# Writing and reading the two halves of one PSUM bank together: a Strassen-type channel layer in four turns instead of five

## The chip, the cores and the metric

The kernel runs on one core of a Trainium2 chip, with five engines that run side by side and meet at semaphores: TensorE (PE in the profile, with its weight loads listed apart as PEld), VectorE (DVE), ScalarE (ACT), GpSimd (POOL) and SyncE (SP), which issues the DMAs. The metric is the device time of one execution in microseconds; less is better.

## The reference

Three layers follow each other, all in fp32: a windowed attention, a gated channel mix, and a block that mixes along the sequence and then along the channels. The change touches only the last of them.

```python
def _moe2_ref(x, U, V, w_ch1, w_ch2) -> np.ndarray:
    xt = x.transpose(0, 2, 1)
    h = xt @ U @ V
    u = x + h.transpose(0, 2, 1)
    ch = np.maximum(u @ w_ch1, 0.0) @ w_ch2
    return (u + ch).astype(np.float32)
```

Here `x` is 4 x 576 x 512, `w_ch1` is 512 x 2048 and `w_ch2` is 2048 x 512. The "first channel layer" is `u @ w_ch1` with its relu, the "second" is the product with `w_ch2`.

## The kernel before

**Products.** Each fp32 product is made of three matmuls in a faster format: an operand is split into a high part (a copy that ACT rounds) and a low part (the rest, a subtraction on DVE or POOL), and high x high, low x high and high x low are added up in PSUM. The helper `part_split` does a split: `part_hi` on ACT, `part_lo` on the engine that it is given.

**Groups and pairs.** The 2304 tokens are cut into one group of 256 (g = 0) and four groups of 512 (g = 1 to 4), the 2048 hidden channels into eight blocks j of 256. The work runs over pairs (g, j), 40 in all, in the order of `VISITS`: four blocks of each group, then all eight of group 4, then the other four blocks of groups 3, 2, 1 and 0. For the 32 pairs with g of 1 or more a pair is a 2 x 2 block product, done by Winograd's form of Strassen's method with seven products of quarter size instead of eight. `ch1(g, j)` makes the first layer of a pair, `ch2(g, j, ...)` the second, one pair later. The eight pairs of group 0 (`ch1_first`) have two products for each layer.

**The first layer of a pair.** Its seven products of six matmuls (128 x 128 by 128 x 256) all go through one PSUM bank of 512 columns, half 0 or half 1 (`at_`). Products are accumulated on top of what the halves hold, and between them DVE or ACT read the partial sums. Before the change each read takes one half (256 columns): `taken` copies product 2 to p2 on ACT; `relu_sum` (line 1264) and `less` (line 1269) on DVE make h11, p5, u2, t3 and h22; the last read is h21 on ACT (line 1292). Then follow sums and splits that make the operands of the second layer.

**The second layer of a pair.** Seven products, each added into its own bank (`ACC`, seven banks), so that of PSUM's eight banks one is left to the first layer. A product is one operation of six matmuls, three for each half m.

**The operands of a group.** Before a visit `x_steps` makes seven operands of the group: three plain blocks (`x_plain`) and the sums T1, T2, T4 and T3 (`x_sum`, `more`), each with a split whose low part runs on POOL (`X_ENG`).

**The order of the work.** All operations are put into a list with the keys that they read and write, and a planner in the kernel (`plan`) simulates them with estimated durations, tries 84 orders and takes the best. An operation of PE is a whole product; the planner puts one where its keys are free. Before the change the keys of the two halves are apart, `(acc, 0)` and `(acc, 1)`. The framework below sets the semaphores by itself, from the tiles that each instruction touches, in the order that the planner wrote.

Of the kernel before, what the change touches and what calls it, by code (L numbers as in the profile page):

```python
# [15 lines left out]
ALU = mybir.AluOpType  # L16
# [3 lines left out]
P = 128  # L20
# [52 lines left out]
LATER = {(0, 0): ((2, 1), (2, 2), (3, 2)), (4, 2): ((4, 1), (4, 2)), (4, 3): ((5, 1), (5, 2)), (4, 4): ((6, 1), (6, 2)), (4, 5): ((7, 1), (7, 2))}  # L73
VISITS = tuple((g, 0, 4) for g in range(4)) + ((4, 0, 8),) + tuple((g, 4, 8) for g in (3, 2, 1, 0))
PRESUM = 6
W_ENG, X_ENG, H_ENG = (("DVE",) * 4, ("DVE",) * 4), "POOL", "DVE"
W_TAG = ("rt k2", "pt pt", "w32 w32")
FLT_MAX = 3.4028235e38
# [23 lines left out]
def tile_attention_mix_channel(  # L102
# [431 lines left out]
    def part_split(eng, x, hi, lo):  # L534
        part_hi(x, hi)
        part_lo(eng, x, hi, lo)
# [86 lines left out]
    def weight(j, layer, name):  # L623

        n, c = (AT1 if layer == 1 else AT2)[name]
        p = wparts[j]
        return cut(p[n, "h"], c, c + Q), cut(p[n, "l"], c, c + Q)
# [526 lines left out]
    def x_plain(g, name, k, t):  # L1154
        x_slot(g, name)
        part_split(X_ENG, ublocks[g, k, t], *operands[g, name])
# [3 lines left out]
    def x_sum(g, name, a, b):  # L1160
        x_slot(g, name)
        t = tt[g, name] = loose("y", 2, "tt")
        part_sum(t, a, b, ALU.subtract)
        part_split(X_ENG, t, *operands[g, name])

    def x_steps(g):

        def ub(k, t):
            return ublocks[g, k, t]

        def more(name, of, last):
            x_slot(g, name)
            t = tt[g, name] = tt[g, last]
            part_sum(t, of, t, ALU.subtract)
            part_split(X_ENG, t, *operands[g, name])

        if g == 0:
            return [
                lambda: (load_block(0, 0, 0), load_block(0, 1, 0)),
                lambda: x_plain(0, "1", 0, 0),  # L1180
                lambda: x_plain(0, "2", 1, 0),
                lambda: x_sum(0, "d", ub(1, 0), ub(0, 0)),
            ]
        return [
            lambda: [load_block(g, k, t) for t, k in ((0, 1), (0, 0), (1, 0), (1, 1))],
            lambda: x_plain(g, "21", 1, 0),
            lambda: x_sum(g, "T1", ub(0, 1), ub(0, 0)),
            lambda: x_plain(g, "11", 0, 0),
            lambda: more("T2", ub(1, 1), "T1"),
            lambda: x_plain(g, "22", 1, 1),  # L1190
            lambda: more("T4", ub(1, 0), "T2"),
            lambda: x_sum(g, "T3", ub(1, 1), ub(0, 1)),
        ]
# [5 lines left out]
    def ch1_bank(g, j):  # L1199
        return fixed_bank("M", 3 if g or j % 2 == 0 else 2)  # L1200

    def ch1_product(g, j, acc, at_, trips, start, keys):

        wx = [(weight(j, 1, w), operands[g, x]) for w, x in trips]

        def run():
            a = acc()[:, at_ * Q : (at_ + 1) * Q]
            n = 0
            for (wh, wl), (xh, xl) in wx:
                for i in range(2):  # L1210
                    ci, wi = (i * Q, (i + 1) * Q), (i * P, (i + 1) * P)
                    n += 1
                    last = n == 2 * len(wx)
                    nc.tensor.matmul(a, lhsT=wh(*wi), rhs=xh(*ci), start=start and n == 1, stop=False, skip_group_check=True)  # L1214
                    nc.tensor.matmul(a, lhsT=wl(*wi), rhs=xh(*ci), start=False, stop=False, skip_group_check=True)  # L1215
                    nc.tensor.matmul(a, lhsT=wh(*wi), rhs=xl(*ci), start=False, stop=last, skip_group_check=True)  # L1216

        r = [k for (wh, wl), (xh, xl) in wx for y in (wh, wl, xh, xl) for k in y.keys()]
        pe(6 * len(wx) * MMQ, run, r + keys[0], [(acc, at_)] + keys[1], "f32r")

    H_LOW = {"a": 0, "b": 2, "t": 4, "c": 5}
    H_HIGH = (
# [8 lines left out]
    def ch1_first(j):  # L1231

        acc = ch1_bank(0, j)
        ch1_product(0, j, acc, 0, (("11", "1"), ("12", "2")), True, ([], [(acc,)]))
        ch1_product(0, j, acc, 1, (("S1", "1"), ("22", "d")), True, ([], [(acc,)]))
        x = {k: part(*v) for k, v in H_FIRST[j % 2].items()}
        pair, t = loose("pr", 2, "hp"), loose("pr", 1, "ht")
        act(2 * Q, lambda: nc.scalar.activation(pair.words(), acc(), AF.Relu), [(acc,), (acc, 0), (acc, 1)], pair.keys(), psum=True)
        part_sum(t, cut(pair, Q, 2 * Q), cut(pair, 0, Q), ALU.subtract)
        part_split(H_ENG, pair, x["ph"], x["pl"])  # L1240
        part_split(H_ENG, t, x["th"], x["tl"])
        return {
            "1": (cut(x["ph"], 0, Q), cut(x["pl"], 0, Q)), "2": (cut(x["ph"], Q, 2 * Q), cut(x["pl"], Q, 2 * Q)), "d": (x["th"], x["tl"])}

    def ch1(g, j):
        if g == 0:
            return ch1_first(j)
        acc = ch1_bank(g, j)
        fresh = (acc, "start")
        hi = {k: part(*v) for k, v in H_HIGH[j % 2].items()}  # L1250
        lo = {k: part("x", j % 2, H_LOW[k], hi[k].n // Q) for k in hi}
        a, b, c, p25 = loose("pr", 2, "ha"), loose("pr", 2, "hb"), loose("sig", 4, "hc"), loose("m", 2, "p25")
        h11, t1, h22, t3 = cut(a, 0, Q), cut(a, Q, 2 * Q), cut(b, 0, Q), cut(b, Q, 2 * Q)
        t2, h21, t4, u2 = (cut(c, i * Q, (i + 1) * Q) for i in range(4))
        p2, p5 = cut(p25, 0, Q), cut(p25, Q, 2 * Q)

        def product(n, at_, start):
            ch1_product(g, j, acc, at_, (USES[n],), start, ([], [fresh, (acc, 0)]) if start else ([fresh], []))

        def taken(to, at_):  # L1260
            copy(Q, lambda: to.words(), lambda: acc()[:, at_ * Q : (at_ + 1) * Q], [(acc, at_)], to.keys(), psum=True)

        def relu_sum(to, at_, more):
            dve(Q, lambda: nc.vector._custom_dve(  # L1264
                TENSOR_ADD_SAT, out=to.words(), in0=acc()[:, at_ * Q : (at_ + 1) * Q], in1=more.words(), s0=FLT_MAX, s1=0.0),
                [(acc, at_)] + more.keys(), to.keys(), two=True, psum=True)

        def less(to, at_, b):
            dve(Q, lambda: nc.vector.tensor_tensor(  # L1269
                out=to.words(), in0=acc()[:, at_ * Q : (at_ + 1) * Q], in1=b.words(), op=ALU.subtract),  # L1270
                [(acc, at_)] + b.keys(), to.keys(), two=True, psum=True)

        product(2, 1, True)
        taken(p2, 1)
        product(1, 0, False)
        relu_sum(h11, 0, p2)
        product(5, 1, False)
        less(p5, 1, p2)
        product(6, 0, False)
        less(u2, 0, p2)  # L1280
        product(3, 1, False)
        relu_sum(t3, 1, u2)
        product(7, 0, False)
        part_sum(t1, t3, h11, ALU.subtract)
        relu_sum(h22, 0, p5)
        product(4, 0, False)
        part_split(H_ENG, a, hi["a"], lo["a"])
        part_sum(t3, h22, t3, ALU.subtract)
        part_sum(t2, h22, t1, ALU.subtract)
        part_split(H_ENG, b, hi["b"], lo["b"])  # L1290
        part_split(H_ENG, t2, hi["t"], lo["t"])
        act(Q, lambda: nc.scalar.activation(h21.words(), acc()[:, :Q], AF.Relu), [(acc, 0)], h21.keys(), psum=True)
        part_sum(t4, h21, t2, ALU.subtract)
        part_split(H_ENG, cut(c, Q, 3 * Q), hi["c"], lo["c"])
        at_ = {"11": ("a", 0), "T1": ("a", 1), "22": ("b", 0), "T3": ("b", 1), "T2": ("t", 0), "21": ("c", 0), "T4": ("c", 1)}
        return {n: tuple(cut(z[k], i * Q, (i + 1) * Q) for z in (hi, lo)) for n, (k, i) in at_.items()}
# [4 lines left out]
    def ch2_product(j, acc, trips, hid, first, last):  # L1301
        wx = [(weight(j, 2, w), hid[x]) for w, x in trips]

        def run():
            for m in range(2):
                a = acc()[:, m * Q : (m + 1) * Q]
                wi = (m * P, (m + 1) * P)
                for i, ((wh, wl), (xh, xl)) in enumerate(wx):
                    start, stop = first and m == 0 and i == 0, last and i == len(wx) - 1
                    nc.tensor.matmul(a, lhsT=wh(*wi), rhs=xh(), start=start, stop=False, skip_group_check=True)  # L1310
                    nc.tensor.matmul(a, lhsT=wl(*wi), rhs=xh(), start=False, stop=False, skip_group_check=True)  # L1311
                    nc.tensor.matmul(a, lhsT=wh(*wi), rhs=xl(), start=False, stop=stop, skip_group_check=True)  # L1312

        r = [k for (wh, wl), (xh, xl) in wx for y in (wh, wl, xh, xl) for k in y.keys()]
        pe(6 * len(wx) * MMQ, run, r, [(acc,)], "f32r")

    def ch2(g, j, hid, first, last, h):
        if g == 0:
# [315 lines left out]
```

## Time and profile before

| | us |
|---|---|
| median of three runs (787.13 to 788.87) | 788.27 |
| the profiled execution, its own time | 785.79 |
| its span in the profile | 783.9 |

The span is what the profile covers, from the first instruction to the last; 1.9 us of the execution lie around it. Matmuls are pipelined, so the profile's busy time of PE counts overlaps, and the distance from one matmul's start to the next says more. The first products of the channel layers start at 343.9 us of the span; from about 400 us on nothing else runs on PE but the two channel layers.

### The profile page before, as it was taken

How to read it: one execution, taken by the hardware profiler on the slowest of the kernel's cores; microseconds unless marked ns; L12 is line 12 of the kernel's file. 1: busy time of each engine (PE TensorE's matmuls, PEld its weight loads, DVE VectorE, ACT ScalarE, POOL GpSimd, SP SyncE). 2: the span in 40 equal slices, each digit the busy share in tenths (PEclk: the TensorE clock that was granted, in tenths of full speed). 3: DMA queues.
4: the chain of work that ended last, by engine and by line, in shares of the span. 5: the costliest groups of instructions: out<-in, count | busy, mean ns of one | idle time of the engine just before them, and what ended most of it. 6: DMA issues, size and time to landing. Idle time of an engine off the chain costs nothing.

```text
span 783.9 us, 19194 instructions
## 1 busy us (share of the span) xinstructions
PE 739.7 (94%) x7498; PEld 697.4 (89%) x7498; DVE 590.5 (75%) x1502; ACT 402.0 (51%) x1017; POOL 202.3 (26%) x219
## 2 busy tenths in 40 slices
PE   8999999999989999988989889999999999989998
PEld 6778999999989999977879879888888899889997
DVE  5879988877676547899866888768887778676853
ACT  6888977676857454745424323244554333243321
POOL 0111555454735341212303013040003113040100
PEclk9999999999999999999999999999999999999999
DMA  9976269777565405576442444512542111303113
GB/s 324 333 271 215 66 217 289 237 237 220 182 199 198 125 2 173 180 218 202 153 150 81 148 154 143 169 61 86 171 142 77 53 41 48 101 14 122 56 41 108
DMA packets 69963, 117.71 MB, mean 150 GB/s; under 512 B 6128, under 2 KB 41200, under 8 KB 69872
## 3 DMA queue, kind: packets, MB, share of 16 engines
q1 hardware_dynamic: 69872, 116.49, 45.5%
q8 instruction: 59, 0.97, 0.5%
q14 instruction: 32, 0.26, 0.1%
HBM read 85.00 MB, written 31.46 MB: 149 GB/s over the span
## 4 chain that ended last, share of the span: by engine, by line
PE 79%; DVE 9%; issue 4%; ACT 3%; DMA 3%; SPq 1%; POOL 0%; DVEq 0%; ACTq 0%; POOLq 0%
PE psM L1214 10%; PE psM L956 9%; PE psM L958 9%; PE psM L957 9%; PE psM L1216 7%; PE psM L1215 7%; PE psM L953 3%; PE psM L1312 3%; PE psM L1310 3%; PE psM L1311 3%; PE psS L1312 3%; PE psS L1310 3%; PE psS L1311 3%; PE psS L873 2%; PE psS L817 2%
## 5 line engine op out<-in xcount | busy, mean ns | idle before, releaser
L956 PE MATMUL psM<-xk,wh 128*128 128x288 f32 x336 | 100.7, 300 | 0.0
L957 PE MATMUL psM<-xk,wl 128*128 128x288 f32 x336 | 99.1, 295 | 0.0
L958 PE MATMUL psM<-xk,wh 128*128 128x288 f32 x336 | 98.9, 294 | 0.0
L1214 PE MATMUL psM<-boxraw,wh 128*128 128x256 f32 x198 | 60.6, 306 | 9.1 <-DVE p L1269 4.8
L1214 PE MATMUL psM<-boxw,wh 128*128 128x256 f32 x186 | 57.0, 307 | 11.4 <-DVE hb L1264 3.4
L956 PE MATMUL psM<-k2s,wh 128*128 128x288 f32 x224 | 67.4, 301 | 0.0
L957 PE MATMUL psM<-k2s,wl 128*128 128x288 f32 x224 | 66.1, 295 | 0.0
L958 PE MATMUL psM<-k2s,wh 128*128 128x288 f32 x224 | 65.9, 294 | 0.0
L385 ACT ACTIVATE boxx<-ha 128x512 fp32r<-128x512 f32 x32 | 20.2, 631 | 86.9 <-DVE ha L541 65.7
L956 PEld LDWEIGHTS psM<-xk,wh 128*128 128x128 f32 x336 | 63.0, 187 | 1.9 <-DVE mn L663 1.4
L957 PEld LDWEIGHTS psM<-xk,wl 128*128 128x128 f32 x336 | 63.1, 188 | 0.1
L958 PEld LDWEIGHTS psM<-xk,wh 128*128 128x128 f32 x336 | 63.2, 188 | 0.0
L380 POOL TENSOR_TENSOR k2s<-k,k2s 128x288 fp32r<-128x288 f32 x49 | 42.9, 877 | 49.6 <-ACT k2s L385 47.2
L1215 PE MATMUL psM<-boxraw,wl 128*128 128x256 f32 x198 | 55.3, 279 | 0.0
L1216 PE MATMUL psM<-boxraw,wh 128*128 128x256 f32 x198 | 55.2, 279 | 0.0
L1312 PE MATMUL psS<-boxx,wh 128*128 128x256 f32 x192 | 54.2, 282 | 0.0
L380 POOL TENSOR_TENSOR xk<-m,xk 128x288 fp32r<-128x288 f32 x48 | 41.4, 871 | 48.0 <-ACT xk L385 29.1
L1215 PE MATMUL psM<-boxw,wl 128*128 128x256 f32 x186 | 51.9, 279 | 0.0
L1216 PE MATMUL psM<-boxw,wh 128*128 128x256 f32 x186 | 51.9, 279 | 0.0
L1214 PEld LDWEIGHTS psM<-boxraw,wh 128*128 128x128 f32 x198 | 37.1, 187 | 15.9 <-DVE p L1269 7.6
L1214 PEld LDWEIGHTS psM<-boxw,wh 128*128 128x128 f32 x186 | 34.8, 187 | 17.4 <-DVE hb L1264 4.4
L672 ACT ACTIVATE pr<-pr,mn 128x64 f32<-128x64 f32 x144 | 47.9, 335 | 3.7 <-DVE mn L663 3.6
(235 smaller groups left out, 2544.4 us busy)
## 6 DMA issues: line engine op xcount, KB each, us to landing
w<-w2raw SPq DMA_DIRECT2D x32, 512.0 KB, 5.4
w<-w1raw SPq DMA_DIRECT2D x20, 512.0 KB, 6.2
w2f<-w SPq DMA_DIRECT2D x32, 256.0 KB, 3.1
ub<-uf SPq DMA_DIRECT2D x32, 256.0 KB, 3.3
ws<-w2f SPq DMA_DIRECT2D x24, 256.0 KB, 3.8
raw<-qk SPq DMA_DIRECT2D x16, 320.0 KB, 5.8
ytmp<-y SPq DMA_DIRECT2D x32, 144.0 KB, 3.2
yb<-ytmp SPq DMA_DIRECT2D x4, 1152.0 KB, 6.8
```

The lines of the kernel that those rows point to most:

```text
L380: op("POOL", t, lambda: nc.gpsimd.tensor_tensor(out=out_(), in0=a(), in1=b(), op=ALU.subtract), r, w, 40, lock=True)
L672: nc.scalar.activation(pr[:, d : d + KW], pr[:, d : d + KW], AF.Exp, bias=mn[:, i : i + 1], scale=-1.0, accum_out=sm[:, i : i + 1])
L953: nc.tensor.matmul(a, lhsT=whole_w[w]()[:, c_], rhs=cols(xw, n_w), start=start, stop=stop)
L956: nc.tensor.matmul(a, lhsT=wh, rhs=xh, start=start, stop=False)
L957: nc.tensor.matmul(a, lhsT=wl, rhs=xh, start=False, stop=False)
L958: nc.tensor.matmul(a, lhsT=wh, rhs=xl, start=False, stop=stop)
L1214: nc.tensor.matmul(a, lhsT=wh(*wi), rhs=xh(*ci), start=start and n == 1, stop=False, skip_group_check=True)
L1215: nc.tensor.matmul(a, lhsT=wl(*wi), rhs=xh(*ci), start=False, stop=False, skip_group_check=True)
L1216: nc.tensor.matmul(a, lhsT=wh(*wi), rhs=xl(*ci), start=False, stop=last, skip_group_check=True)
L1310: nc.tensor.matmul(a, lhsT=wh(*wi), rhs=xh(), start=start, stop=False, skip_group_check=True)
L1311: nc.tensor.matmul(a, lhsT=wl(*wi), rhs=xh(), start=False, stop=False, skip_group_check=True)
L1312: nc.tensor.matmul(a, lhsT=wh(*wi), rhs=xl(), start=False, stop=stop, skip_group_check=True)
```

## The change

The two halves of the bank become one key. `ch1_products` writes up to two products, one for each half, as one operation of PE: (2, 1), then (5, 6), then (3, 7), then (4). Between these turns the whole bank of 512 columns is read at once: by a copy on ACT into `pq`, by a copy on ACT into `ux`, by one `relu_sum` on DVE into `b` (which gives h22 and t3), and at the end by the relu on ACT into h21 as before. What DVE computed from PSUM is now computed from the two copies in SBUF: h11, and two differences. In the second layer an operation is three matmuls instead of six. The low parts of T1, T2, T4 and T3 move from POOL to DVE (`T_ENG`), and the block "11" is split ahead of T1.

```diff
+T_ENG = "DVE"
...
         part_sum(t, a, b, ALU.subtract)
-        part_split(X_ENG, t, *operands[g, name])
+        part_split(T_ENG, t, *operands[g, name])
...
             lambda: x_plain(g, "21", 1, 0),
+            lambda: x_plain(g, "11", 0, 0),
             lambda: x_sum(g, "T1", ub(0, 1), ub(0, 0)),
-            lambda: x_plain(g, "11", 0, 0),
...
-    def ch1_product(g, j, acc, at_, trips, start, keys):
-
-        wx = [(weight(j, 1, w), operands[g, x]) for w, x in trips]
+    def ch1_products(g, j, acc, what):
+
+        sums = [(at_, start, [(weight(j, 1, w), operands[g, x]) for w, x in trips]) for at_, start, trips in what]
...
+        pairs = [x for _, _, wx in sums for x in wx]
+        r = [k for (wh, wl), (xh, xl) in pairs for y in (wh, wl, xh, xl) for k in y.keys()]
+        pe(6 * len(pairs) * MMQ, run, r, [(acc,)], "f32r")
...
-        product(2, 1, True)
-        taken(p2, 1)
-        product(1, 0, False)
-        relu_sum(h11, 0, p2)
-        product(5, 1, False)
-        less(p5, 1, p2)
-        product(6, 0, False)
-        less(u2, 0, p2)
-        product(3, 1, False)
-        relu_sum(t3, 1, u2)
-        product(7, 0, False)
+        products((2, 1), (1, 0))
+        taken(pq)
+        products((5, 1), (6, 0))
+        relu_sum(h11, lambda: p1.words(), p1.keys(), p2)
+        taken(ux)
+        part_sum(p1, cut(ux, Q, 2 * Q), p2, ALU.subtract)
+        part_sum(p2, cut(ux, 0, Q), p2, ALU.subtract)
+        products((3, 1), (7, 0))
+        relu_sum(b, lambda: acc(), [(acc,)], pq, psum=True)
+        products((4, 0))
         part_sum(t1, t3, h11, ALU.subtract)
-        relu_sum(h22, 0, p5)
-        product(4, 0, False)
...
-        pe(6 * len(wx) * MMQ, run, r, [(acc,)], "f32r")
+        for m in range(2):
+            pe(3 * len(wx) * MMQ, lambda m=m: run(m), r, [(acc,)], "f32r")
```

## Rows read from the trace of the kernel before

**Rows 1.** The page: engines over the span, granted clock, chain that ended last.

```profile
PE 739.7 (94%) x7498; PEld 697.4 (89%) x7498; DVE 590.5 (75%) x1502; ACT 402.0 (51%) x1017; POOL 202.3 (26%) x219
...
PEclk9999999999999999999999999999999999999999
...
PE 79%; DVE 9%; issue 4%; ACT 3%; DMA 3%; SPq 1%; POOL 0%; DVEq 0%; ACTq 0%; POOLq 0%
```

**Rows 2.** Busy time by stretch: start and end, length, engines (instructions), clock, DMA.

```profile
400.00:784.00 384.00, 354.46 (x2790) 337.93 (x2788) 281.90 (x576) 138.84 (x280) 60.44 (x44) 1.00 0.31 98
344.00:784.00 440.00, 403.31 (x3144) 381.62 (x3142) 331.79 (x674) 166.38 (x334) 72.80 (x53) 1.00 0.35 109
```

**Rows 3.** Waits of PE's weight loads: total us, times, longest.

```profile
PEld psM L1214 <- DVE p L1269: 13.5, 22, 1.1
PEld psM L1214 <- DVE hb L1264: 10.8, 16, 1.7
PEld psM L1214 <- DVE ha L1264: 5.8, 8, 0.8
PEld psM L1214 <- DVE hc L1269: 5.1, 10, 0.7
PEld psM L1214 <- ACT p L385: 4.6, 13, 0.7
...
PEld psM L1214 <- ACT hp L1238: 2.0, 2, 1.8
PEld psM L1214 <- ACT hc L1292: 1.5, 3, 0.7
```

**Rows 4.** Timeline of one pair: start, length, engine, line, [idle before <- releaser].

```profile
567.58 0.37 ACT L385 ACTIVATE p<-psM 128x256 f32<-128x256 f32 x1
...
568.00 0.39 PE L1214 MATMUL psM<-boxw,wh 128*128 128x256 f32 x1
568.23 0.28 PE L1215 MATMUL psM<-boxw,wl 128*128 128x256 f32 x1
...
569.41 0.28 PE L1216 MATMUL psM<-boxw,wh 128*128 128x256 f32 x1
...
569.73 0.42 DVE L1264 CUSTOM_DVE_ANT_0 ha<-psM,p 128x256 f32<-128x256 f32 x1 [0.51 <-PE psM L1216]
...
570.07 0.41 DVE L1269 TENSOR_TENSOR p<-psM,p 128x256 f32<-128x256 f32 x1
...
570.54 0.38 PE L1214 MATMUL psM<-boxraw,wh 128*128 128x256 f32 x1
...
572.25 0.42 DVE L1269 TENSOR_TENSOR hc<-psM,p 128x256 f32<-128x256 f32 x1 [0.57 <-PE psM L1216]
...
572.78 0.34 PE L1214 MATMUL psM<-boxraw,wh 128*128 128x256 f32 x1
...
574.09 0.68 DVE L382 TENSOR_TENSOR wl<-ws,wh 128x512 fp32r<-128x512 f32 x1
574.69 0.42 DVE L1264 CUSTOM_DVE_ANT_0 hb<-psM,p 128x256 f32<-128x256 f32 x1
...
575.16 0.38 PE L1214 MATMUL psM<-boxraw,wh 128*128 128x256 f32 x1 [0.74 <-DVE hb L1264]
```

**Rows 5.** Timeline of ACT, one read of the bank behind a split.

```profile
556.77 0.62 ACT L385 ACTIVATE boxB<-hb 128x512 fp32r<-128x512 f32 x1
557.29 0.36 ACT L385 ACTIVATE p<-psM 128x256 f32<-128x256 f32 x1
```

**Rows 6.** Groups by line and shape: count, busy us, mean ns, idle before.

```profile
L1238 ACT ACTIVATE hp<-psM 128x512 f32<-128x512 f32 x8 | 4.8, 594 | 8.8 <-PE psM L1216 8.8
L1344 DVE TENSOR_TENSOR ui<-psS,ui 128x512 f32<-128x512 f32 x28 | 19.0, 682 | 0.6 <-PE psS L1312 0.4
```

**Rows 7.** The tile of the sums T: duration ns least/median/longest, first and last start.

```profile
L380 POOL TENSOR_TENSOR boxw<-tt,boxw x14: 1271/1302/1797, 353.7 to 698.3; 128x512 fp32r<-128x512 f32 x14
L541 DVE TENSOR_TENSOR tt<-ub,tt x14: 679/688/1779, 372.1 to 696.8; 128x512 f32<-128x512 f32 x14
```

More of the change, by code (lines that the diff above doesn't have):

```diff
@@ L1174, in more @@
             part_sum(t, of, t, ALU.subtract)
-            part_split(X_ENG, t, *operands[g, name])
+            part_split(T_ENG, t, *operands[g, name])
         if g == 0:
@@ L1200, in ch1_bank @@
         return fixed_bank("M", 3 if g or j % 2 == 0 else 2)
-    def ch1_product(g, j, acc, at_, trips, start, keys):
-        wx = [(weight(j, 1, w), operands[g, x]) for w, x in trips]
+    def ch1_products(g, j, acc, what):
+        sums = [(at_, start, [(weight(j, 1, w), operands[g, x]) for w, x in trips]) for at_, start, trips in what]
         def run():
[L1207 to L1219, printed above, removed]
+            for at_, start, wx in sums:
+                a = acc()[:, at_ * Q : (at_ + 1) * Q]
+                n = 0
+                for (wh, wl), (xh, xl) in wx:
+                    for i in range(2):
+                        ci, wi = (i * Q, (i + 1) * Q), (i * P, (i + 1) * P)
+                        n += 1
+                        last = n == 2 * len(wx)
+                        nc.tensor.matmul(a, lhsT=wh(*wi), rhs=xh(*ci), start=start and n == 1, stop=False, skip_group_check=True)
+                        nc.tensor.matmul(a, lhsT=wl(*wi), rhs=xh(*ci), start=False, stop=False, skip_group_check=True)
+                        nc.tensor.matmul(a, lhsT=wh(*wi), rhs=xl(*ci), start=False, stop=last, skip_group_check=True)
+        pairs = [x for _, _, wx in sums for x in wx]
+        r = [k for (wh, wl), (xh, xl) in pairs for y in (wh, wl, xh, xl) for k in y.keys()]
+        pe(6 * len(pairs) * MMQ, run, r, [(acc,)], "f32r")
     H_LOW = {"a": 0, "b": 2, "t": 4, "c": 5}
@@ L1233, in ch1_first @@
         acc = ch1_bank(0, j)
-        ch1_product(0, j, acc, 0, (("11", "1"), ("12", "2")), True, ([], [(acc,)]))
-        ch1_product(0, j, acc, 1, (("S1", "1"), ("22", "d")), True, ([], [(acc,)]))
+        ch1_products(0, j, acc, [(0, True, (("11", "1"), ("12", "2")))])
+        ch1_products(0, j, acc, [(1, True, (("S1", "1"), ("22", "d")))])
         x = {k: part(*v) for k, v in H_FIRST[j % 2].items()}
         pair, t = loose("pr", 2, "hp"), loose("pr", 1, "ht")
-        act(2 * Q, lambda: nc.scalar.activation(pair.words(), acc(), AF.Relu), [(acc,), (acc, 0), (acc, 1)], pair.keys(), psum=True)
+        act(2 * Q, lambda: nc.scalar.activation(pair.words(), acc(), AF.Relu), [(acc,)], pair.keys(), psum=True)
         part_sum(t, cut(pair, Q, 2 * Q), cut(pair, 0, Q), ALU.subtract)
@@ L1248, in ch1 @@
         acc = ch1_bank(g, j)
-        fresh = (acc, "start")
         hi = {k: part(*v) for k, v in H_HIGH[j % 2].items()}
         lo = {k: part("x", j % 2, H_LOW[k], hi[k].n // Q) for k in hi}
-        a, b, c, p25 = loose("pr", 2, "ha"), loose("pr", 2, "hb"), loose("sig", 4, "hc"), loose("m", 2, "p25")
+        a, b, c, pq = loose("pr", 2, "ha"), loose("pr", 2, "hb"), loose("sig", 3, "hc"), loose("m", 2, "pq")
         h11, t1, h22, t3 = cut(a, 0, Q), cut(a, Q, 2 * Q), cut(b, 0, Q), cut(b, Q, 2 * Q)
-        t2, h21, t4, u2 = (cut(c, i * Q, (i + 1) * Q) for i in range(4))
@@ L1255, in ch1 @@
[L1255 to L1271, printed above, removed]
-        product(2, 1, True)
-        taken(p2, 1)
-        product(1, 0, False)
-        relu_sum(h11, 0, p2)
-        product(5, 1, False)
-        less(p5, 1, p2)
-        product(6, 0, False)
-        less(u2, 0, p2)
-        product(3, 1, False)
@@ L1282, in ch1, with products, taken, relu_sum @@
-        relu_sum(t3, 1, u2)
-        product(7, 0, False)
+        t2, h21, t4 = (cut(c, i * Q, (i + 1) * Q) for i in range(3))
+        p1, p2, ux = cut(pq, 0, Q), cut(pq, Q, 2 * Q), cut(c, 0, 2 * Q)
+        def products(*what):
+            ch1_products(g, j, acc, [(at_, n == 2, (USES[n],)) for n, at_ in what])
+        def taken(to):
+            copy(to.n, lambda: to.words(), lambda: acc(), [(acc,)], to.keys(), psum=True)
+        def relu_sum(to, x, x_keys, more, psum=False):
+            dve(to.n, lambda: nc.vector._custom_dve(
+                TENSOR_ADD_SAT, out=to.words(), in0=x(), in1=more.words(), s0=FLT_MAX, s1=0.0),
+                x_keys + more.keys(), to.keys(), two=True, psum=psum)
@@ L1291, in ch1 @@
         part_split(H_ENG, t2, hi["t"], lo["t"])
-        act(Q, lambda: nc.scalar.activation(h21.words(), acc()[:, :Q], AF.Relu), [(acc, 0)], h21.keys(), psum=True)
+        act(Q, lambda: nc.scalar.activation(h21.words(), acc()[:, :Q], AF.Relu), [(acc,)], h21.keys(), psum=True)
         part_sum(t4, h21, t2, ALU.subtract)
@@ L1302, in ch2_product, with run @@
         wx = [(weight(j, 2, w), hid[x]) for w, x in trips]
[L1304 to L1312, printed above, removed]
+        def run(m):
+            a = acc()[:, m * Q : (m + 1) * Q]
+            wi = (m * P, (m + 1) * P)
+            for i, ((wh, wl), (xh, xl)) in enumerate(wx):
+                start, stop = first and m == 0 and i == 0, last and i == len(wx) - 1
+                nc.tensor.matmul(a, lhsT=wh(*wi), rhs=xh(), start=start, stop=False, skip_group_check=True)
+                nc.tensor.matmul(a, lhsT=wl(*wi), rhs=xh(), start=False, stop=False, skip_group_check=True)
+                nc.tensor.matmul(a, lhsT=wh(*wi), rhs=xl(), start=False, stop=stop, skip_group_check=True)
         r = [k for (wh, wl), (xh, xl) in wx for y in (wh, wl, xh, xl) for k in y.keys()]
-        pe(6 * len(wx) * MMQ, run, r, [(acc,)], "f32r")
+        for m in range(2):
+            pe(3 * len(wx) * MMQ, lambda m=m: run(m), r, [(acc,)], "f32r")
     def ch2(g, j, hid, first, last, h):
```

## The prediction

> **What bounds the kernel now.** I read the page first. PE is busy 94% of the span, its clock is full in every slice, and the chain that ended last runs 79% of its time through PE, 9% through DVE [rows 1]. So the time is PE's: its matmuls, and the stretches where it waits. How long one matmul really takes is seen in the timeline: from 568.23 to 569.41 there are ten steps, 0.118 us each, while the listed durations are 0.28 [rows 4]. The second view is busy time by stretch. From 400 us to the end there are 2790 matmuls [rows 2]; 2790 x 0.118 = 329 us, and the stretch is 384 us long. So about 55 us of this stretch are not matmuls (a little less, if some records are missing). The busy share hides that.
>
> The third view says where they are: the waits of the weight loads, which stop when PE stops. All the large ones stand before line 1214, the first matmul of a first-layer product: 13.5 + 10.8 + 5.8 + 5.1 = 35.2 us for DVE, 4.6 + 1.5 = 6.1 us for ACT, 2.0 us for the relu of group 0 [rows 3], 43.3 us in all. Second-layer products wait for nothing worth a row.
>
> The fourth view, the timeline of one pair, says why. Product 2 has been written; ACT copies p2 at 567.58; at 568.00 PE goes on with products 1 and 5, twelve matmuls [rows 4]. Product 1 is in half 0 and ends in the middle of these, near 568.7. Yet DVE reads h11 from half 0 only at 569.73, after 0.51 us idle, when product 5 in the other half is also done. It then takes p5 at 570.07, and PE starts again at 570.54 [rows 4]. So the halves do not work in turns: a write in one keeps a reader of the other out, and the reader keeps PE out. The planner, whose keys hold the halves apart, does not know it, and puts only one second-layer product (6 x 0.118 = 0.71 us) into a turnaround that takes 569.41 + 0.118 = 569.53 to 570.54, 1.01 us: 0.30 us lost. The next one (u2 at 572.25) takes no longer than the product that covers it, and PE restarts at 572.78. The one after has two reads, t3 and h22, with a weight split of 0.68 us at 574.09 between them, and h22 at 574.69 lets PE go at 575.16 after 0.74 us of idle [rows 4]. A pair thus has five turns: (2), (1, 5), (6, 3), (7), (4).
>
> A restart costs a little more: after a wait the second matmul comes 0.23 us after the first (568.00 to 568.23) instead of 0.118, and 0.11 lost is the most that I see. At 0.08 us on average (my choice; the bounds are 0 and 0.11) and 32 x 5 = 160 turns that is 13 us. The sum is 43 + 13 = 56 us, against the 55 from the stretch. This is all that the change can reach.
>
> **The change part by part.**
>
> *Four turns instead of five, known to the planner.* The seven products stay, 42 matmuls a pair, and nothing is gained there. Restarts: 32 x 4 = 128 x 0.08 = 10 us, 3 us less. The turnarounds become longer. A copy of 512 columns from PSUM on ACT has the row of group 0's relu, 0.594 us [rows 6]. In front of it stands the delay from PE's last matmul to the reader, 569.53 to 569.73 = 0.20 us, and behind it 567.58 + 0.37 = 567.95 to 568.00, 0.05 us [rows 4]: 0.85 us. The read on DVE is not in the trace with 512 columns; the nearest row is the bank sum of line 1344, 0.682 us [rows 6]: 0.20 + 0.68 + 0.05 = 0.93 us. The last read, 256 columns on ACT: 0.20 + 0.37 + 0.05 = 0.62 us.
>
> *Units of three matmuls.* A unit covers 3 x 0.118 = 0.354 us. The four turnarounds need 3 + 3 + 3 + 2 = 11 units, and a pair has 14. Seven undivided products would cover four turnarounds too (2 + 2 + 2 + 1 = 7), with nothing over, so the units matter for the choice and cost PE nothing: the matmuls and weight loads are the same ones.
>
> *What stays of the waits.* Of the turns DVE closes 32 instead of 96. Today's mean is 35.2 / 96 = 0.37 us; at the same mean 32 x 0.37 = 12 us stay, and 0 if the plan covers them. Reads on DVE still stand behind other work of DVE, so I take 8. ACT's reads are 96 (two copies and h21) instead of 64; at today's 6.1 / 64 = 0.095 us that is 9 us, and I keep it. Group 0 keeps its 2 us. With the restarts: 8 + 9 + 2 + 10 = 29 us in place of 56, a gain of 27.
>
> *Work for DVE and ACT.* ACT copies 1024 columns a pair instead of 256: 2 x 0.594 - 0.37 = 0.82 us, 26 us over 32 pairs. From 344 us on ACT is busy 166 of 440 us [rows 2], so it has the room; what its queue does to the reads is a rival below. On DVE h11 and the two differences keep their size and come from SBUF, and h22 and t3 become one instruction. The 30 low parts of the sums T that leave POOL (1.30 us each there) cost DVE about one split of 0.68 us each [rows 7, 4]: 20 us. DVE is busy 332 of 440 us [rows 2], 108 us are free, and a group's operands are made a visit ahead. That idle time is the cover; without it up to 20 us would come back. A split falls in front of one of the 32 reads with a chance of about 20 / 440: under 1 us, and I take 1. On the other side each operand is ready 0.6 us sooner, at no visible gain. The DMAs are the same ones from the same queue; that "11" is split ahead of T1 moves one split on ACT and POOL and no transfer: nothing.
>
> From the Trainium skill one rule speaks against this part. SBUF — State Buffer, section "Who interferes with whom", says that a DVE instruction with two inputs in SBUF contends with a GpSimd instruction that reads SBUF, and that the one that comes second is blocked for the whole of the other. The change gives DVE 3 x 32 = 96 such instructions that had one input in PSUM, and it takes 30 instructions from POOL. The trace agrees: a sum on `tt` took 1779 ns at the longest and 688 at the median, a POOL split 1797 against 1302 [rows 7]. By the rule POOL is left busy about 34 of 440 us, 8%, so that some 8 of the 96 would wait up to 1.3 us: at most 10 us of DVE time, which the same idle time covers. The sum is the same with it or without.
>
> **The sum.** 27 - 1 = 26 us. The profiled execution took 785.8 us, which gives 759.8; the median of the runs is 2.5 us above it, so I predict 762.3 us.
>
> **Rivals.**
>
> *Nearly all waits go.* A planner that knows the bank covers every turnaround; only restarts stay, and at the lower bounds not all of those. Gain 37 to 47 us: 741 to 751. For it: 14 units for 11. Against it: the reads stand in queues with other work on both engines.
>
> *The turnarounds eat it.* The units run out because the operands of the pair before come late: with h22 and t3 read last, the sums, four low parts (3 x 0.68 + 0.42) and the rest, some 4 us of DVE, all lie behind the third turn. Then PE idles once a pair for up to a turnaround without cover, 0.85 us; 32 x 0.85 = 27 us, which takes back a half to all of the gain: 772 to 788. Against it: the waits of the weight loads hold no second-layer product of any size [rows 3].
>
> *The copies stand behind ACT's splits (slower).* Each of the 64 copies is in ACT's one queue. In the trace a read of the bank at 557.29 comes only after a split of 0.62 us that began at 556.77 [rows 5]. Three units cover 1.06 us, a turnaround of 0.85 has 0.21 to spare. One split ahead of each copy costs 0.62 - 0.21 = 0.41 us, 64 x 0.41 = 26 us, and that is exactly the point from which the change decides against itself; two splits ahead cost 1.03 us, 66 us, and the time is 788 + 40 = 828. One and a half gives 808. Against it: today's 64 reads of ACT lose 0.095 us each, and ACT is busy 38% of the stage.
>
> *The change does nothing*, if the planner's new order ends up as tight as the old one: 787 to 790. The order of all other work is drawn anew as well; no row prices that, and it may be a few us either way.
>
> **How the numbers follow.** My forecast, a gain of 16 to 36 us, has 0.54; nearly all waits gone 0.15; a half to all eaten 0.15, of which 0.12 still faster by over 0.2%; nothing 0.03; copies behind splits 0.13. Two tenths of a per cent are 1.6 us, about what three runs can tell here. Faster: 0.54 + 0.15 + 0.12 = 0.81; same 0.06; slower 0.13. The range for 8 in 10 leaves out the slower case and the very best: 744 to 788. The likeliest case alone spans 752 to 772.
>
> **What would show it.** Right: the waits of line 1214's weight loads (now the helper's new line) fall from 43 us to about 19; bursts of twelve first-layer matmuls with three units of three between them; the reads of the bank are 512 columns, about 0.6 us on ACT and 0.68 on DVE; POOL has 30 fewer splits; the stretch from 400 us on is some 25 us shorter, the part before 344 us as long as now. Wrong: waits for ACT's copies of tens of us; second-layer matmuls that wait for low parts on DVE; or a first part that differs by more than 5 us.

## The result and the profile after

The changed kernel takes 738.77 us (median of four runs, 736.63 to 739.85) against 787.70 us for the kernel before beside it: a ratio of 0.9381, interval 0.9346 to 0.9415. It is faster by 49 us where 26 were forecast, and the time lies below the range that was given.

The page of the changed kernel, in the lines that answer to [rows 1]: engines over the span, granted clock, chain that ended last.

```profile
span 738.1 us, 19229 instructions
...
PE 721.8 (98%) x7514; PEld 695.3 (94%) x7514; DVE 596.5 (81%) x1500; ACT 424.6 (58%) x1049; POOL 164.5 (22%) x189
...
PEclk9999999999999999999999999999999999999999
```

PE's matmuls are as many as before but for 16, and its span is 45.8 us shorter: what went is idle time. Busy time by stretch, as [rows 2]:

```profile
400.00:738.00 338.00, 332.68 (x2793) 331.24 (x2791) 289.67 (x571) 158.77 (x310) 27.96 (x19) 1.00 0.36 112
344.00:738.00 394.00, 385.20 (x3183) 379.79 (x3181) 344.77 (x679) 189.45 (x370) 34.08 (x23) 1.00 0.39 122
```

From 400 us to the end 2793 matmuls at 0.118 us make 330 of 338 us; 8 us are left that are no matmul, where the kernel before had 55 (384 us with 2790 matmuls). About 4 us of either lie behind the last matmul, which starts at 733.76 here and at 779.86 before. These 47 us account for all of the 45.8 us between the two spans; the medians of the runs lie 49 us apart. The waits of the weight loads, as [rows 3]:

```profile
PEld psM L1216 <- DVE hb L1266: 3.1, 4, 1.7
...
PEld psM L1216 <- ACT hc L1286: 1.6, 2, 0.8
...
PEld psM L1216 <- ACT hc L386: 0.3, 1, 0.3
PEld psM L1216 <- ACT boxw L386: 0.2, 1, 0.2
```

43.3 us have become 5.2. A turnaround of the changed kernel, as [rows 4], without some of the matmuls between:

```profile
511.96 0.68 DVE L1266 CUSTOM_DVE_ANT_0 hb<-psM,pq 128x512 f32<-128x512 f32 x1
...
518.88 0.28 PE L1218 MATMUL psM<-boxraw,wh 128*128 128x256 f32 x1
519.00 0.28 PE L1303 MATMUL psS<-boxB,wh 128*128 128x256 f32 x1
...
519.20 0.60 ACT L386 ACTIVATE hc<-psM 128x512 f32<-128x512 f32 x1 [1.55 <-PE psM L1218]
...
519.93 0.28 PE L1305 MATMUL psS<-boxx,wh 128*128 128x256 f32 x1
520.05 0.28 PE L1216 MATMUL psM<-boxraw,wh 128*128 128x256 f32 x1
...
520.29 0.28 PE L1218 MATMUL psM<-boxraw,wh 128*128 128x256 f32 x1
```

The turn ends with the matmul at 518.88; ACT reads the whole bank from 519.20 to 519.80; PE does nine second-layer matmuls, three units, and starts the next turn at 520.05. From there to the matmul two further on it is 0.24 us, two plain steps: the wait is over before PE comes to it, and there is no restart to pay. The reads have the forecast lengths (the copy 0.60 us, the read on DVE 0.68).

### The profile page after: what moved, and what is told of

Read it like the earlier page. It is cut to its first block, busy times and chain, and to the rows that moved or that the text cites. A ratio compares the mean times of both kernels' runs of the same rounds, so it can differ in the third digit from the quotient of the medians.

```text
span 738.1 us, 19229 instructions
## 1 busy us (share of the span) xinstructions
PE 721.8 (98%) x7514; PEld 695.3 (94%) x7514; DVE 596.5 (81%) x1500; ACT 424.6 (58%) x1049; POOL 164.5 (22%) x189
## 4 chain that ended last, share of the span: by engine, by line
PE 83%; DVE 8%; ACT 3%; issue 2%; DMA 2%; SPq 1%; DVEq 0%; ACTq 0%
PE psM L957 10%; PE psM L959 10%; PE psM L958 10%; PE psM L1216 7%; PE psM L1218 7%; PE psM L1217 7%; PE psS L1303 4%; PE psS L1305 4%; PE psS L1304 4%; PE psM L1303 3%; PE psM L1305 3%; PE psM L1304 3%; PE psM L954 3%; PE psS L874 2%; PE psS L818 2%
## 5 line engine op out<-in xcount | busy, mean ns | idle before, releaser
L381 POOL TENSOR_TENSOR boxw<-ub,boxw 128x512 fp32r<-128x512 f32 x13 | 19.7, 1520 | 179.8 <-ACT boxw L386 154.0
L1216 PE MATMUL psM<-boxraw,wh 128*128 128x256 f32 x198 | 56.1, 283 | 0.6 <-ACT hc L1286 0.5
L1216 PE MATMUL psM<-boxw,wh 128*128 128x256 f32 x186 | 53.5, 288 | 2.3 <-DVE hb L1266 1.5
L1218 PE MATMUL psM<-boxraw,wh 128*128 128x256 f32 x198 | 55.2, 279 | 0.0
L1218 PE MATMUL psM<-boxw,wh 128*128 128x256 f32 x186 | 52.0, 280 | 0.4 <-DVE boxw L383 0.4
L381 POOL TENSOR_TENSOR xk<-m,xk 128x288 fp32r<-128x288 f32 x48 | 43.2, 913 | 40.7 <-ACT xk L386 31.7
L381 POOL TENSOR_TENSOR boxraw<-ub,boxraw 128x512 fp32r<-128x512 f32 x12 | 17.7, 1479 | 140.7 <-ACT boxraw L386 87.4
L1019 DVE SCALAR_TENSOR_TENSOR k<-psM,rt 128x288 f32<-128x288 f32 x56 | 25.5, 456 | 25.8 <-ACT rt L1014 24.6
```

What stands on the lines that cost most here:

```text
L381: op("POOL", t, lambda: nc.gpsimd.tensor_tensor(out=out_(), in0=a(), in1=b(), op=ALU.subtract), r, w, 40, lock=True)
L1019: dve(HS, lambda: nc.vector.scalar_tensor_tensor(out=k2(), in0=acc()[:, :HS], scalar=0.0, in1=rt(), op0=ALU.max, op1=ALU.mult), [(acc,), k ...
```

## The experiments

All times are medians of runs beside the kernel before on the same chip; the ratio is against that kernel.

**1. The units alone.** The kernel before with the last part of the change:

```diff
-        pe(6 * len(wx) * MMQ, run, r, [(acc,)], "f32r")
+        for m in range(2):
+            pe(3 * len(wx) * MMQ, lambda m=m: run(m), r, [(acc,)], "f32r")
```

> The kernel before with one part of the change alone: second-layer operations of three matmuls instead of six. Theory A (the planner's books: its keys hold the two halves of the bank apart, so it leaves turnarounds too short, whatever the size of a unit): the waits before the first matmul of a first-layer product stay near 43 us of weight-load idle, and the time is 780 to 792 us. Theory C (the size of a unit decides: six matmuls are too coarse to fill a turnaround): most of the gain comes with the units alone, 745 to 760 us.

787.62 us, ratio 1.0007 (0.9995 to 1.0019). A finer unit is worth nothing where the planner does not know how long it has to fill.

**2. The units of six again in the changed kernel**, the same lines turned back.

> The changed kernel with second-layer operations of six matmuls again, the four turns on the whole bank kept. Theory A: the planner knows the turnarounds of 0.85 to 0.93 us and wants two products of 0.71 us in each of three, and one in the fourth, 7 of 7, so nearly all waits stay away: 739 to 750 us. Theory C: 765 to 785 us. Theory D (whole-bank reads and fewer turns are what counts, not the books): like A, so this run alone does not tell A from D.

748.92 us, ratio 0.9510 (0.9487 to 0.9532). Without the units 10 us of the 49 are missing; the rest of the change, with T on DVE, keeps 38.

**3. T on POOL in the changed kernel.**

```diff
-T_ENG = "DVE"
+T_ENG = "POOL"
```

> The changed kernel with the low parts of the sums T on GpSimd again. If the move to VectorE is a side matter (my prediction: under 1 us, hidden by 108 us of VectorE's idle time): 736 to 742 us. Rival: in the tighter stage a split of 1.3 us on GpSimd delays a group's operands at the start of a visit and holds VectorE's sums: 743 to 752 us.

748.24 us, ratio 0.9496 (0.9470 to 0.9522): the rival. Some 6 of the 9.5 us are lost in one place, the start of group 4's visit, which the last section shows.

**4. The key alone: the planner knows the bank, five turns, reads of 256 columns,** units of six, T on POOL.

```diff
+        products((2, 1))
+        taken(p2, 1)
+        products((1, 0), (5, 1))
+        relu_sum(h11, 0, p2)
+        less(p5, 1, p2)
+        products((6, 0), (3, 1))
+        less(u2, 0, p2)
+        relu_sum(t3, 1, u2)
+        products((7, 0))
+        relu_sum(h22, 0, p5)
+        products((4, 0))
```

Every product and every read has the one key `(acc,)`. Against the kernel before two more things differ: the products of a turn are one operation of PE, and the block "11" is split first. Experiment 8 has the early "11" (with T on DVE) and finds it worth nothing; the key was not run without the joined products.

> The planner's keys made one for the whole bank, but the reads as in the kernel before (256 columns each, five turns: 2; 1 and 5; 6 and 3; 7; 4), products of six matmuls, T on GpSimd. Theory A: knowing the bank is most of the gain; the turnarounds of 0.62 to 1.0 us ask for 1 + 2 + 2 + 1 + 1 = 7 of 7 products, which fits only just: 745 to 765 us. Theory D (four turns with whole reads make the gain): 775 to 790 us.

772.33 us, ratio 0.9808 (0.9786 to 0.9831), between the two expectations. Of the 55 us that are no matmul 43 are left (371 us from 400 us on, 2782 matmuls). The waits of its weight loads:

```profile
PEld psM L1216 <- DVE hb L1266: 24.4, 32, 1.4
PEld psM L1216 <- ACT hc L1292: 5.2, 7, 0.7
```

The waits for h11 and p5 are no longer among the larger ones; those for t3 and h22, both in `hb`, are now the largest.

**5. The key and the units**, the same kernel with units of three.

> The five-turn kernel with one key for the bank (772.3 us) and second-layer operations of three matmuls as well; reads of 256 columns, T on GpSimd. Theory A+C (the books and the units together make the gain): the turnarounds ask for 2 + 3 + 3 + 2 + 2 = 12 units of 14, so nearly all waits go: 745 to 755 us. Theory D (four turns with whole reads are needed): 765 to 775 us, and the waits for VectorE's reads stay near 20 us.

763.16 us, ratio 0.9690 (0.9662 to 0.9718), between the two expectations. The waits for `hb` did fall, from 24.4 to 6.5 us, but those behind the last read, for the next pair's first turn, rose from 5.2 to 9.1, and the time is only 2 us below what theory D gave: the books and the units together make half of the gain. The units are worth 9 us here.

```profile
PEld psM L1216 <- ACT hc L1292: 9.1, 11, 1.6
PEld psM L1216 <- DVE hb L1266: 6.5, 11, 1.4
```

**6 and 7. Another seed of the planner**, once with T on DVE, once on POOL.

```diff
-SEED = 1
+SEED = 2
```

> The changed kernel with another seed of the planner's random orders: nothing else differs. If the gain is the turns' and not a lucky order: 735 to 750 us. If the draw decides several per cent: beyond that. It is the measure for all differences of about 1% between the other runs.

> T's low parts on GpSimd (748.2 us with the first seed) with the other seed. If their place costs about 9 us by itself, through late operands at the start of the visit of group 4 where PE stalled and its clock fell: about 9 us above the run with the same seed and T on VectorE. If the 9 us were the draw: within 3 us of that run.

738.36 us (ratio 0.9367, 0.9330 to 0.9404) and 742.65 us (0.9429, 0.9402 to 0.9457). The changed kernel does not hang on the draw. The place of T's low parts is worth 4 us with this seed and 9 with the other, so the 9 are partly the draw.

**8. T on DVE in the kernel before**, and "11" split first.

> The kernel before with the low parts of T on VectorE and the block 11 split first, nothing else. My prediction's price: 0 to 1 us lost, 784 to 790 us. Rival (the operands of a visit are late in the kernel before too): 775 to 782 us.

787.08 us, ratio 0.9985 (0.9968 to 1.0001): nothing, as forecast for this kernel.

**9. The four turns with whole reads alone**: the changed kernel with units of six (as in 2) and T on POOL (as in 3).

> The four turns with whole-bank reads alone: second-layer operations of six matmuls, T on GpSimd. If the parts add up (units 10 us, T 9.5 us by the runs that undo one of them): 758 us. If both undoings hit the same stall at the start of group 4's visit: 748 to 753 us.

762.31 us, ratio 0.9663 (0.9641 to 0.9685); both expectations were too low. The parts do not add up: from here the units alone give 14 us (748.24), T alone 13 (748.92), both 24 (738.77). In its busy time by stretch the clock is below full in three stretches before 500 us:

```profile
344.00:400.00 56.00, 48.38 (x331) 43.85 (x330) 47.90 (x87) 27.07 (x52) 13.31 (x10) 0.94 0.52 167
400.00:450.00 50.00, 47.12 (x378) 46.30 (x378) 42.70 (x84) 20.91 (x42) 9.80 (x7) 0.97 0.42 137
450.00:500.00 50.00, 46.20 (x370) 45.26 (x370) 45.41 (x89) 20.97 (x40) 11.45 (x8) 0.97 0.51 164
500.00:550.00 50.00, 49.39 (x414) 49.12 (x414) 43.15 (x86) 24.16 (x49) 8.31 (x6) 1.00 0.43 138
```

**10. Four turns, reads of 256 columns** from PSUM, in the changed kernel:

```diff
+        products((2, 1), (1, 0))
+        taken(p2, 1)
+        relu_sum(h11, 0, p2)
+        products((5, 1), (6, 0))
+        less(u2, 0, p2)
+        less(p5, 1, p2)
+        products((3, 1), (7, 0))
+        relu_sum(t3, 1, u2)
+        relu_sum(h22, 0, p5)
+        products((4, 0))
```

> The changed kernel (units of three, T on VectorE, one key) with the four turns, but every read takes 256 columns from PSUM as before: p2 on ScalarE, then h11; u2 and p5; t3 and h22 on VectorE. Turnarounds of about 1.15, 1.0 and 1.0 us ask for 4 + 3 + 3 + 2 = 12 units of 14. If the number of turns is what counts: 737 to 745 us. If the copies of the whole bank on the idle ScalarE count: 750 to 765 us, with waits for VectorE's reads.

743.82 us, ratio 0.9430 (0.9404 to 0.9455). 11 us of its stretch are no matmul (340 us, 2788 matmuls) against 8. So the number of turns is most of what turns and reads give (the table below has 15 us of 20); the 5 us between it and the changed kernel, whose interval overlaps this one, are not sure.

**11. A shorter booked latency**: the planner counts 100 ns instead of 300 from the end of a first-layer turn.

```diff
-        pe(6 * len(pairs) * MMQ, run, r, [(acc,)], "f32r")
+        pe(6 * len(pairs) * MMQ, run, r, [(acc,)], "f32r", 100)
```

> The changed kernel in which the planner books 100 ns instead of 300 ns from the end of a first-layer turn to its reader. The trace of before shows 200 ns. My explanation for the vanished restarts is that the planned 300 ns puts a unit more into each turnaround than the reader needs, so that the semaphore is up before PE arrives. If so, this plan has one unit less (6 matmuls in most turnarounds), the waits and restarts come back, and the time is 750 to 765 us. If the margin is not the cause: 736 to 742 us.

748.50 us, ratio 0.9488 (0.9462 to 0.9514); 10 us back, a little less than expected. Its waits, and the start of a turn in its timeline:

```profile
PEld psM L1216 <- ACT pq L386: 3.9, 22, 0.2
PEld psM L1216 <- ACT hc L386: 3.7, 20, 0.2
```

```profile
513.55 0.28 PE L1305 MATMUL psS<-boxx,wh 128*128 128x256 f32 x1
...
513.67 0.36 PE L1216 MATMUL psM<-boxw,wh 128*128 128x256 f32 x1
...
513.88 0.28 PE L1217 MATMUL psM<-boxw,wl 128*128 128x256 f32 x1
...
514.00 0.28 PE L1218 MATMUL psM<-boxw,wh 128*128 128x256 f32 x1
```

There are 42 waits of 0.2 us behind ACT's copies now, and restarts even where PE did not idle: 0.21 us from 513.67 to 513.88, then 0.12. From 400 us on 71 turns have a second matmul that is over 0.04 us late, by 6.8 us in all, against 27 turns and 2.3 us in the changed kernel with the same four turns a pair. What took the restarts away is that the semaphore is up before PE needs it.

**12. A longer one, 500 ns.**

> The changed kernel with 500 ns booked from the end of a first-layer turn to its reader instead of 300. The turnarounds already hold 9 matmuls and no wait. If the units suffice for a fourth unit: 737 to 741 us. If they run out (4 x 3 + 3 = 15 of 14): 742 to 755 us, with some turnarounds that have no unit left.

746.65 us, ratio 0.9486 (0.9462 to 0.9510): the units run out. What waits is the next pair's first turn:

```profile
PEld psM L1216 <- ACT hc L1286: 8.5, 16, 1.2
```

**13. A longer booked latency without the knowledge**: the kernel before with units of three, its keys apart, and 700 ns.

```diff
-        pe(6 * len(wx) * MMQ, run, r + keys[0], [(acc, at_)] + keys[1], "f32r")
+        pe(6 * len(wx) * MMQ, run, r + keys[0], [(acc, at_)] + keys[1], "f32r", 700)
```

> The kernel before with units of three and its keys for the halves kept apart, but 700 ns booked after each first-layer product instead of 300. If a longer booked turnaround is all that the knowledge of the bank gives: 763 to 775 us, as the five-turn kernels that know the bank (772.3 and 763.2 us). If the planner must know that the two halves block each other: 780 to 792 us.

813.86 us, ratio 1.0343 (1.0308 to 1.0378), slower than both expected. Its waits:

```profile
PEld psM L1214 <- ACT p L385: 19.0, 29, 0.7
PEld psM L1214 <- DVE p L1269: 18.8, 30, 0.9
PEld psM L1214 <- DVE hb L1264: 12.2, 19, 1.4
```

PE now stands 29 times behind ACT's copy of p2. One of them in the timeline:

```profile
605.29 0.28 PE L1216 MATMUL psM<-boxw,wh 128*128 128x256 f32 x1
...
606.69 0.28 PE L1216 MATMUL psM<-boxw,wh 128*128 128x256 f32 x1
607.01 0.38 ACT L385 ACTIVATE p<-psM 128x256 f32<-128x256 f32 x1 [1.00 <-PE psM L1216]
607.44 0.38 PE L1214 MATMUL psM<-boxw,wh 128*128 128x256 f32 x1 [0.47 <-ACT p L385]
```

Product 2 ends with the matmul at 605.29, and six second-layer matmuls do stand behind it, enough for the copy. But in the planner's books product 1, in the other half, does not depend on the copy, so both are due when the 700 ns are over. The copy idles until product 1 has ended at 606.69, and product 5, right behind product 1 and with nothing between, waits for the copy. A later read only meets the next write. A margin is no substitute for the right key. How much of the 26 us by which this is worse than before comes from this meeting was not tried.

**14. Five turns, units of three, T on DVE**, to have the turns against the changed kernel with all else equal.

> Five turns with reads of 256 columns, one key, units of three, T on VectorE: against the changed kernel (738.8 us) it differs only in the turns and reads, against the run with T on GpSimd (763.2 us) only in T. If the number of turns is the larger part: 755 to 764 us. If T on VectorE is what made the changed kernel fast: 740 to 750 us.

758.95 us, ratio 0.9639 (0.9615 to 0.9662): the turns and reads are worth 20 us, T on DVE 4.

**15. The plain blocks' low parts on DVE too**, in the changed kernel.

```diff
-W_ENG, X_ENG, H_ENG = (("DVE",) * 4, ("DVE",) * 4), "POOL", "DVE"
+W_ENG, X_ENG, H_ENG = (("DVE",) * 4, ("DVE",) * 4), "DVE", "DVE"
```

> The changed kernel with the low parts of the plain blocks on VectorE too (25 splits of 0.68 us, 17 us more). If late operands at the start of a visit are what is left: 732 to 737 us. If VectorE, over 90% busy between 500 and 600 us in the changed kernel, becomes the bound: 740 to 750 us.

740.15 us, ratio 0.9396 (0.9369 to 0.9422): no change beside the changed kernel. No run beat it clearly.

**16. The kernel before with the other seed.**

> The kernel before with the other seed of the planner's random orders: 783 to 793 us if the draw is worth little; it tells how far the 787.6 us of the units alone and the kernel before are a lucky or unlucky order.

788.32 us, ratio 1.0001 (0.9979 to 1.0022).

Put one after another, with all times beside about 787 us for the kernel before:

| step | us | gain | no matmul after 400 us |
|---|---|---|---|
| the kernel before | 787 | | 55 |
| one key, five turns | 772.3 | 15 | 43 |
| units of three | 763.2 | 9 | 33 |
| T on DVE | 759.0 | 4 | 28 |
| four turns | 743.8 | 15 | 11 |
| whole reads, two of them on ACT | 738.8 | 5 | 8 |

The last column is the stretch from 400 us to the end less its matmuls at 0.118 us. For the four rows between the first and the last, in order:

```profile
400.00:771.00 371.00, 343.56 (x2782) 333.56 (x2781) 274.85 (x577) 134.10 (x280) 59.79 (x44) 1.00 0.33 101
400.00:761.00 361.00, 344.59 (x2784) 336.25 (x2782) 279.97 (x576) 133.80 (x280) 60.87 (x44) 0.99 0.33 104
400.00:757.00 357.00, 344.26 (x2786) 334.93 (x2784) 287.92 (x601) 134.00 (x280) 25.67 (x19) 1.00 0.34 104
400.00:740.00 340.00, 334.46 (x2788) 332.08 (x2786) 287.74 (x600) 136.87 (x280) 25.94 (x19) 1.00 0.35 109
```

The rows are from different chips, each beside its own kernel before, and the gain of each depends on those taken before it (experiments 2, 3 and 9), so the table is one way of dividing the 49 us and not the only one.

## Why the prediction was wrong, step by step

*Where the time was: right, but for 4 us.* Of the 55 us about 4 lie behind the last matmul, where the change cannot reach. Summed from one matmul's start to the next, the turns of the kernel before have 37 us of waits and 12 us of restarts; the estimate was 43 and 13. 47 of the 55 us went.

*That the halves exclude each other and the planner does not know it: right, and shown* by experiments 4 and 13. One key, with the products of a turn joined, brings 15 us with the same number of turns and reads of 256 columns. The planner's own end time says the same. Worked out from the sources of the kernels, with an order that is that of the traces matmul for matmul, it is 734 us for the kernel before and 742 for experiment 13, whose spans are 783.9 and 811.0; with the one key it is 766 for experiment 4 and 732 for the changed kernel, and the spans are 771.0 and 738.1. With the old books the planner's end was 50 to 69 us too early, with the new ones 5 to 6. Plan against plan, the change is worth 2 us; its gain is that the plan comes true. The Trainium skill has a rule that bears on it: PSUM — Partial Sum Buffer, section "PSUM bank collisions raise a hardware error", wants PSUM guarded by bank and quadrant, not by address. The trace agrees in so far as this program's semaphores guard so: the reader of one half idled 0.51 us until the other half was written [rows 4]. What happens without the guard no run here shows.

*The turnarounds: right.* 0.85 us for a copy was the estimate; 518.88 + 0.118 to 519.80 is 0.80, without the 0.05 us behind it. The read on DVE took the 0.68 us that its 0.93 were built on. Three units cover each.

*"What stays of the waits": the step that failed.* I carried today's means over: 8 us for DVE, 9 for ACT, 2 for group 0, 10 for restarts, 29 in all, where 8 are left. The 8 hold the 4 us behind the last matmul, which the 29 do not. The means of before (0.37 us for a read on DVE, 0.095 on ACT) were those of a plan that took a read to be free of the other half; a plan that knows better covers the reads, and DVE keeps 3.1 us instead of 8, ACT 2.1 instead of 9, group 0 nothing worth a row instead of 2. The restarts I took for a price of every turn, 10 us. They are a price of arriving early: 125 turns of the kernel before pay them, 27 of the changed one (2.3 us), and experiment 11 brings them back with the same turns. My rival "nearly all waits go" was the case, with 0.15 for a chance, and its lower end of 741 us was still 2 us too high.

*The units: mis-sized.* I booked them at nothing and let them only help the plan. That is right alone (experiment 1); together with the turns they are worth 9 to 14 us (experiments 2, 5 and 9).

*T on DVE: wrong in sign.* I took 1 us of loss and saw "no visible gain" in operands that are ready sooner. In the kernel before that holds (experiment 8). In the changed kernel the start of a visit is the next thing that is late, and the move is worth 4 to 9 us, 13 with units of six (experiments 3, 7, 14 and 9). I had asked what hides the cost and not what becomes late once the other waits are gone.

*DVE with two inputs in SBUF.* Up to 10 us of DVE time were the estimate. In the changed kernel, the tile `pq`:

```profile
L542 DVE TENSOR_TENSOR pq<-hc,pq x64: 409/422/1535, 389.6 to 695.3; 128x256 f32<-128x256 f32 x64
...
L1266 DVE CUSTOM_DVE_ANT_0 ha<-pq x32: 411/420/1414, 387.6 to 693.3; 128x256 f32<-128x256 f32 x32
```

The longest took 1.5 us against 0.42. PE saw little of it: its waits for DVE before first-layer products are 3.1 us in all.

*Slower, by copies behind ACT's splits: did not come.* ACT's copies cost PE 0.3 us.

## What to carry to other kernels

Where a planner or a hand-made order decides what fills a wait, first compare its dependencies with those that the trace shows: a reader that idles until an unrelated half is written says that the model is wrong, and a finer fill or a longer margin bought nothing or less than nothing here until it was put right. When most waits of a stage go, do not carry their means over to what stays; ask what covers each, and look at what was off the path (here the operands at the start of a visit), since a cost that was truly nothing before can be a per cent after. And compare the end that the plan gives for itself with the measured one: here a gap of 50 us in the kernel before held nearly the whole gain.

## What the runs showed of the hardware

**A restart after a wait costs about 0.1 us even without idle time.** If the semaphore comes up late, the second matmul stands 0.21 to 0.23 us behind the first instead of 0.118 in the rows shown (experiment 11 and [rows 4]); if it is up early, there is nothing (520.05 to 520.29 above). I took this for a fixed price of a dependency.

**After a short starvation PE's granted clock stood at half, and the two are most of what T on POOL costs with the first seed.** At the start of group 4's visit in experiment 3, the timeline and then the busy time by stretch (PE, PEld, DVE, ACT and POOL with their counts, then the clock):

```profile
468.00 1.61 POOL L381 TENSOR_TENSOR boxraw<-tt,boxraw 128x512 fp32r<-128x512 f32 x1 [6.39 <-ACT boxraw L386]
...
468.44 1.45 DVE L1266 CUSTOM_DVE_ANT_0 ha<-pq 128x256 f32<-128x256 f32 x1
...
476.85 0.38 PE L1216 MATMUL psM<-boxw,wh 128*128 128x256 f32 x1 [0.63 <-ACT boxw L386]
...
478.20 0.39 PE L1218 MATMUL psM<-boxw,wh 128*128 128x256 f32 x1 [0.85 <-POOL boxw L381]
...
480.95 0.58 PE L1216 MATMUL psM<-boxraw,wh 128*128 128x256 f32 x1 [2.02 <-DVE hb L1266]
481.33 0.41 PE L1217 MATMUL psM<-boxraw,wl 128*128 128x256 f32 x1
481.55 0.41 PE L1218 MATMUL psM<-boxraw,wh 128*128 128x256 f32 x1
```

```profile
476.00:478.00 2.00, 0.71 (x4) 0.30 (x3) 2.00 (x5) 0.63 (x1) 1.13 (x1) 1.00 0.66 171
478.00:480.00 2.00, 0.74 (x4) 0.53 (x4) 2.00 (x5) 0.00 (x0) 0.14 (x1) 1.00 0.61 206
480.00:482.00 2.00, 1.05 (x5) 1.05 (x6) 2.00 (x6) 0.40 (x1) 0.00 (x0) 0.53 0.89 306
482.00:484.00 2.00, 1.47 (x7) 1.17 (x7) 1.46 (x5) 1.53 (x5) 0.00 (x0) 0.50 0.93 318
484.00:486.00 2.00, 2.00 (x11) 2.00 (x11) 1.75 (x3) 0.42 (x1) 0.00 (x0) 0.50 0.50 137
486.00:488.00 2.00, 2.00 (x15) 2.00 (x14) 1.03 (x2) 1.12 (x2) 0.71 (x1) 0.76 0.25 95
...
466.00:490.00 24.00, 19.96 (x142) 19.06 (x141) 19.32 (x36) 9.26 (x17) 7.09 (x5) 0.86 0.51 158
```

The same stretch of the changed kernel:

```profile
466.00:490.00 24.00, 23.31 (x194) 22.90 (x194) 23.71 (x51) 10.15 (x20) 1.29 (x1) 1.00 0.46 148
```

PE does four matmuls in each of two stretches of 2 us while it waits for an operand of the new group (ACT's copy, POOL's low part) and for DVE. Then the granted clock stands at 0.50, 1.2 GHz, and the step between matmuls is 0.21 to 0.22 us, also from 484 to 486 us, when PE is busy throughout. From 466 to 490 us this kernel does 142 matmuls and the changed one, whose clock stays at 1.00, does 194: 52 x 0.118 = 6.1 us of the 9.5 between the two. The steps tell the two apart: some 20 of them at 0.21 to 0.22 us, until 486.93, make about 2 us, and the waits make the rest. The rows at 468 us show DVE blocked behind POOL: 1.45 us for what takes 0.42, and it ends just after POOL does (468.00 + 1.61 = 469.61, 469.89). The Trainium skill names this lock in SBUF — State Buffer, section "Who interferes with whom", and the rows agree with it.
